# Splitting the Fourier input into halves: reading rows in place and writing with a step, through a small buffer

## The chip, the cores and the metric

The kernel runs on one core of a Trainium2 chip. The metric is the device time of one execution in microseconds (us), taken as the median of several runs.

## The reference

For each of 8 batches of 4224 tokens by 192 channels, a causal convolution with 7 taps per head comes first; it is followed by a two-dimensional Fourier transform of which the real part is kept, a residual sum, a layer norm and a two-layer MLP.

```python
out = np.einsum('hk,bskhg->bshg', w, x_unf)        # w: softmax over the 7 taps of each of 8 heads
x = out.reshape(B, S, D)                           # 8, 4224, 192
X = np.fft.fft(np.fft.fft(x, axis=1), axis=2)
u = x + np.real(X)
un = (u - mu) / np.sqrt(var + 1e-06)               # mu, var over the 192 channels
return u + np.maximum(un @ w_ch1, 0.0) @ w_ch2     # 192 -> 768 -> 192
```

## The kernel before, in words

Almost every matrix product is made of three or five float16 products: a number is split into an upper half (its float16 rounding) and a lower half (what is left, again float16), so that float32 accuracy comes out of float16 matmuls.

**Stages of one batch.** The convolution (`conv_unit`, L440) reads windows of the input, multiplies them by a band matrix and stores the result to a scratch tensor `sc` in DRAM. `load_x` (L530) reads the scratch back as `xs`, 128 partitions by 33 rows of 192 channels, in eight pieces of 4 or 5 rows (`PIECES`, L38): piece 1 has 5 rows, the others have 4. `split_x` (L581) splits a piece into the halves `XH` and `XL`. `stage_a` (L605) multiplies 128-column slices of `XH` and `XL` by the Fourier matrix `F` and evicts `yh` and `yl`. `stage_b` (L630) does the next transform and evicts `V`. `prep` (L715) does the last transform, adds the residual `u`, and computes the layer norm, mostly on POOL. `mlp_hidden` (L839) and `mlp_out` (L863) are the MLP; the first evicts `hh` on ACT (L858) and `hlo` on DVE (L859) out of two PSUM buffers with the tag `h`, the second adds its result to `u` on DVE (L885).

**The split before.** For a piece of n rows of 192 channels, a channel being `t*64 + j` with t in 0..2 and j in 0..63, ACT (L591) multiplies by the batch's scale and writes float16 to `XH`; DVE (L599) then reads `xs` and `XH` and writes the lower half to `XL`. Both walk in the order of `XH`, which is j outside and the 99 numbers (row, t) inside: each instruction writes runs of 12 (or 15) neighbouring float16 numbers and reads float32 numbers that lie 64 elements apart, 256 bytes. An instruction has 768 elements a partition (960 for piece 1).

**Order of the work.** The MLP of the 72 steps (8 batches of 9) sets the pace. The stages of later batches are spread between its units by `front` (L939): the splits of batch 2 and later fall into four steps, two pieces in each, well before the batch's `stage_a`; batch 1 has its own tighter tables (`conv_1` to `a_1`, L931 to L934). `in_turn` (L831) queues an ACT instruction behind the last `hh` eviction emitted before it. Within such limits the framework orders each engine's instructions by a simulated run, in which an engine takes the earliest one in the program that is ready. Each engine then executes its own list strictly in order.

**The head of the program.** For batch 0 there is no MLP to hide behind. `load_first_x` (L549) loads `xs` in four DMAs into the tiles `xs_yh` and `xs_yl`. A tiny POOL copy, `landed` (L578), waits for the last one, and the first residual gathers on POOL (L688) are ordered behind it. For pieces 4 to 7 `split_x` also issues three matmuls into a scratch tile called `idle` (L595), which read that piece's share of `XH`. Then `stage_a` of batch 0 runs; all its matmuls need all eight pieces.

**Buffers.** A tag is a set of slots that tiles share in turn. The tag `hlo` has two slots, used in the head for two input windows and later for the MLP's lower halves. The tag `xl` has one slot, used from batch 2 on by `split_windows` (L403) for the lower half of an input window.

Of the kernel before, what the change touches and what calls it, by code (L numbers as in the profile page):

```python
# [10 lines left out]
F16 = mybir.dt.float16  # L11
# [4 lines left out]
AF = mybir.ActivationFunctionType  # L16
ALU = mybir.AluOpType
# [11 lines left out]
NA, NB, NJ, ND = 128, 33, 64, 3  # L29
NBD = NB * ND  # L30
# [99 lines left out]
def kernel(  # L130
# [13 lines left out]
    nc = tc.nc  # L144
    PSUM = bass.MemoryType.PSUM
    cp = ctx.enter_context(tc.tile_pool(name="cp", bufs=1))
    sb = ctx.enter_context(tc.tile_pool(name="sb", bufs=2))
# [377 lines left out]
    XH = cp.tile([NA, NJ * NBD + 32], F16, name="XH")  # L525
    XL = cp.tile([NA, NJ * NBD + 32], F16, name="XL")
# [53 lines left out]

    def split_x(bt, i):  # L581
        b0, b1 = PIECES[i]
        src = bt.xs.pop(i)[:, : b1 - b0].rearrange("p b (t j) -> p j (b t)", t=ND)

        def part(x):
            return x[:, : NJ * NBD].rearrange("p (j f) -> p j f", f=NBD)[
                :, :, ND * b0 : ND * b1
            ]

        with in_turn():  # L590
            split = nc.scalar.activation(part(XH), src, AF.Copy, scale=bt.c)  # L591
        if bt.b == 0 and i > 3:
            idle = ps.tile([128, HID // 3 * 2], F32, tag="h", name=f"idle_{i}", bufs=2)
            for w in range(3):
                nc.tensor.matmul(  # L595
                    idle[: ND * (b1 - b0)], XH[:, ND * b0 : ND * b1],
                    W1[:, w % 2, : HID // 3 * 2], start=True, stop=True,
                )
        nc.vector.scalar_tensor_tensor(  # L599
            part(XL), src, bt.c, part(XH), op0=ALU.mult, op1=ALU.subtract  # L600
        )
        return split.ins

# [227 lines left out]
    def in_turn():  # L831

        return tc.issue_after(anchor[0]) if anchor[0] else ExitStack()
# [105 lines left out]
    def front(bt, rel):  # L939
        units = []  # L940
        conv, load, split, a = (
            (conv_1, load_1, split_1, a_1) if bt.b == 1
            else (conv_at, load_at, split_at, a_at)
        )
        if bt.b > 1 and rel == min(conv):
            units += [call(split_windows, bt, 0), call(load_windows, bt, 2)]
        for ch in conv.get(rel, ()):
            if bt.b > 1 and ch != conv[rel][0]:
                units += [pause, pause]
            units += [call(conv_unit, bt, ch, p) for p in range(3)]  # L950
            if bt.b > 1 and ch + 1 < NCH:
                units.append(call(split_windows, bt, ch + 1))
            if bt.b > 1 and ch + 3 < NCH:
                units.append(call(load_windows, bt, ch + 3))
        if bt.b > 1 and rel in (min(conv) - 2, min(conv) - 1):
            units.append(call(load_windows, bt, rel - min(conv) + 2))
        if rel == max(conv) - 1 and bt.b >= NB0:
            units.append(call(conv_segments, bt))
        if rel == max(conv) + (bt.b > 1):
            units.append(call(scales, bt))  # L960
        loads = [call(load_x, bt, ch) for ch in load.get(rel, ())]
        splits = [call(split_x, bt, i) for i in split.get(rel, ())]
        for i in range(max(len(loads), len(splits))):
            units += splits[i : i + 1] + loads[i : i + 1]
        units += [call(stage_a, bt, t) for t in a.get(rel, ())]
        return units
# [42 lines left out]
    for i in range(NPC):  # L1009
        split_x(first, i)  # L1010
# [72 lines left out]
    with after(leading["hi"]), after(leading["lo"]):  # L1083
# [3 lines left out]
            op0=ALU.mult, op1=ALU.subtract,  # L1087
        )
    for n in range(len(steps) + 1):
        bt, it = steps[n] if n < len(steps) else (None, 0)  # L1090
# [94 lines left out]
```

## Time and profile before

| what | value |
|---|---|
| three runs | 1221.82, 1225.08, 1227.69 us; median 1225.08 |
| the profiled execution's own time | 1225.67 us |
| its span, first to last instruction | 1223.9 us |
| mean granted TensorE clock | 0.977 |
| busy: PE, DVE, POOL, ACT | 95%, 73%, 66%, 52% |
| instructions of the split: ACT L591, DVE L599 | 64 each |

Engines are named as in the profile: PE is TensorE, DVE VectorE, ACT ScalarE, POOL GpSimd, SP SyncE. "PEclk" is the granted TensorE clock as a share of full speed. A group's row gives the engine, the operation, the tiles out<-in, the shape, the number of instructions, then the busy time in us and the mean ns of one, and last the idle time of the engine just before them and what ended it. In a timeline the first two numbers are the start and the duration in us, and a bracket holds the idle time before and what ended it.

### The profile page before, as it was taken

How to read it: one execution, taken by the hardware profiler on the slowest of the kernel's cores; microseconds unless marked ns; L12 is line 12 of the kernel's file. 1: busy time of each engine (PE TensorE's matmuls, PEld its weight loads, DVE VectorE, ACT ScalarE, POOL GpSimd, SP SyncE). 2: the span in 40 equal slices, each digit the busy share in tenths (PEclk: the TensorE clock that was granted, in tenths of full speed). 3: DMA queues.
4: the chain of work that ended last, by engine and by line, in shares of the span. 5: the costliest groups of instructions: out<-in, count | busy, mean ns of one | idle time of the engine just before them, and what ended most of it. 6: DMA issues, size and time to landing. Idle time of an engine off the chain costs nothing.

```text
span 1223.9 us, 31068 instructions
## 1 busy us (share of the span) xinstructions
PE 1157.8 (95%) x12544; PEld 913.5 (75%) x12544; DVE 894.4 (73%) x2124; ACT 637.6 (52%) x1020; POOL 803.5 (66%) x1104
## 2 busy tenths in 40 slices
PE   4389889999999999999999999999999899999998
PEld 4187668867878778787878778787787777787776
DVE  6767496787767977687867877668778787566543
ACT  5665366555655455654655556554555454333222
POOL 0218965499827896389755897278862899577940
PEclk9589999999999999999999999999999999999999
DMA  8963785474655547384764748466474643323521
GB/s 301 263 187 94 187 184 146 101 182 106 181 142 151 149 126 172 105 191 114 167 170 91 179 105 180 137 153 149 121 175 115 155 106 76 78 69 90 74 56 43
DMA packets 238368, 170.55 MB, mean 139 GB/s; under 512 B 119368, under 2 KB 221968, under 8 KB 238224
## 3 DMA queue, kind: packets, MB, share of 16 engines
q1 hardware_dynamic: 184744, 109.95, 37.4%
q10 hardware_dynamic: 46952, 45.24, 13.2%
q0 software_dynamic: 6528, 13.38, 4.5%
q8 instruction: 98, 1.61, 0.5%
q14 instruction: 46, 0.38, 0.1%
HBM read 83.82 MB, written 58.55 MB: 116 GB/s over the span
## 4 chain that ended last, share of the span: by engine, by line
PE 78%; DVE 8%; DMA 6%; ACT 3%; issue 2%; POOL 1%; SPq 1%; ACTq 0%; DVEq 0%; POOLq 0%
PE ph L854 31%; PE po L879 9%; PE po L873 9%; PE po L876 9%; PE pa L616 6%; PE pq L739 5%; PE pb L642 4%; PE pc L465 4%; DMA xs<-sc 3%; ACT XH L591 2%; DVE XL L599 1%; DMA sc<-xa 1%; DVE yl L625 1%; DMA xs_yl<-sc 1%; PE pc L470 1%
## 5 line engine op out<-in xcount | busy, mean ns | idle before, releaser
L854 PE MATMUL ph<-kt,W 128*128 128x512 f16 (+1 forms) x2160 | 497.9, 363 | 13.8 <-DVE hlo L859 13.3
L858 ACT ACTIVATE hh<-ph 128x512 f16<-128x512 f32 (+1 forms) x400 | 236.5, 593 | 375.7 <-PE ph L854 364.3
L873 PE MATMUL po<-W,hh 128*128 128x192 f16 x1584 | 384.8, 247 | 7.1 <-DVE u L885 7.1
L879 PE MATMUL po<-W,hlo 128*128 128x192 f16 x1584 | 385.3, 247 | 0.0
L876 PE MATMUL po<-W,hh 128*128 128x192 f16 x1584 | 384.7, 247 | 0.0
L859 DVE SCALAR_TENSOR_TENSOR hlo<-ph,hh 128x512 f16<-128x512 f32 (+1 forms) x400 | 269.1, 675 | 122.4 <-ACT hh L858 121.0
L854 PEld LDWEIGHTS <-W 128*128 128x128 f16 x2160 | 192.8, 98 | 153.6 <-issue 15.2
L794 POOL TENSOR_SCALAR un<-u,mv,y 128x192 f32<-128x192 f32 x260 | 280.9, 1088 | 7.8
L876 PEld LDWEIGHTS <-hh 128*128 128x128 f16 x1584 | 155.1, 98 | 28.7 <-issue 8.8
L688 POOL DMA_INDIRECT u<-sc,rows_sb x136 | 155.0, 1140 | 31.4 <-issue 31.2
L873 PEld LDWEIGHTS <-hh 128*128 128x128 f16 x1584 | 155.0, 98 | 23.1 <-issue 0.6
L879 PEld LDWEIGHTS <-hlo 128*128 128x128 f16 x1584 | 155.1, 98 | 18.4 <-issue 0.3
L811 POOL TENSOR_TENSOR hl<-un,hl 128x512 f16<-128x512 f32 (+2 forms) x142 | 131.5, 947 | 5.6
L599 DVE SCALAR_TENSOR_TENSOR XL<-xs,s_x,XH 128x768 f16<-128x768 f32 (+1 forms) x56 | 92.6, 1653 | 43.1 <-ACT XH L591 43.1
L785 POOL TENSOR_SCALAR v<-mv 128x4 f32<-128x4 f32 (+1 forms) x71 | 18.5, 261 | 157.7 <-DVE mv L765 153.4
L757 DVE SCALAR_TENSOR_TENSOR u<-pq,g,u 128x128 f32<-128x128 f32 (+1 forms) x328 | 102.9, 378 | 25.1 <-PE pq L739 20.6
L591 ACT ACTIVATE XH<-xs,s_x 128x768 f16<-128x768 f32 (+1 forms) x56 | 93.9, 1678 | 27.4 <-DMA xs<-sc 27.4
L624 ACT ACTIVATE yh<-pa 99x512 f16<-99x512 f32 x128 | 75.4, 596 | 53.5 <-PE pa L616 43.9
L625 DVE SCALAR_TENSOR_TENSOR yl<-pa,yh 99x512 f16<-99x512 f32 x128 | 85.7, 680 | 23.7 <-ACT yh L624 23.3
L885 DVE SCALAR_TENSOR_TENSOR u<-po,fo,u 128x384 f32<-128x384 f32 (+1 forms) x136 | 80.9, 595 | 27.4 <-PE po L879 26.7
L616 PE MATMUL pa<-c_sb,XH 128*128 128x128 f16 x1024 | 99.6, 221 | 0.0
L739 PE MATMUL pq<-c_sb,V 128*128 128x130 f16 (+1 forms) x1440 | 97.6, 216 | 0.6 <-ACT V L651 0.6
(152 smaller groups left out, 1685.8 us busy)
## 6 DMA issues: line engine op xcount, KB each, us to landing
out_dram<-u SPq DMA_DIRECT2D x64, 384.0 KB
xt<-in_xw_dram ACTq DMA_DIRECT2D x30, 576.0 KB
sc<-xa ACTq DMA_DIRECT2D x30, 540.0 KB
xs<-sc SPq DMA_DIRECT2D x28, 288.0 KB
u<-sc SPq DMA_DIRECT2D x72, 96.0 KB
xt<-in_xw_dram SPq DMA_DIRECT2D x10, 576.0 KB
sc<-xa SPq DMA_DIRECT2D x10, 540.0 KB
xs<-sc SPq DMA_DIRECT2D x28, 192.0 KB
```

Source lines behind the costliest of these rows:

```text
L591: split = nc.scalar.activation(part(XH), src, AF.Copy, scale=bt.c)
L616: nc.tensor.matmul(pa[:, i], x[:, at], F[:, l], start=(n == 0), stop=(n == 2))
L688: nc.gpsimd.indirect_dma_start(to, None, bt.sc[:S], bass.IndirectOffsetOnAxis(ap=rows_sb[:, col : col + 1], axis=0),)
L739: mm = nc.tensor.matmul(po, weights(v, ND * r + k3), rhs[:, 0] if it == Q0 else rhs, start=(r + n == 0), stop=(r == 1 and n == 2),)
L794: (nc.vector if b + it == 0 else nc.gpsimd).tensor_scalar(un[:, g], u[:, g], mv[:, g, 0:1], y[:, g : g + 1], op0=ALU.subtract, op1=ALU.mult,)
L811: lower = (nc.vector if b + it == 0 else nc.gpsimd).tensor_tensor(bl[:, :, o : o + n], un[:, :ng, f], hi[:, :, f], op=ALU.subtract)
L854: nc.tensor.matmul(ph[:, n], W1[:, w, ht * 128 : (ht + 1) * 128], kt[:, k], start=(i == 0), stop=(i == len(order) - 1),)
L858: anchor[0] = nc.scalar.activation(hh, ph, AF.Relu).ins
L859: nc.vector.scalar_tensor_tensor(hlo, ph, 0.0, hh, op0=ALU.max, op1=ALU.subtract)
L873: nc.tensor.matmul(po[:, g % 2], hh[:, ht, tk], W2[:, ht, 0], start=(ht == 0), stop=False)
L876: nc.tensor.matmul(po[:, g % 2], hh[:, ht, tk], W2[:, ht, 1], start=False, stop=False)
L879: nc.tensor.matmul(po[:, g % 2], hlo[:, ht, tk], W2[:, ht, 0], start=False, stop=(ht == 5),)
```

## The change

`split_x` alone is changed. Batch 1 keeps the old form. For the other batches:

- ACT's scaled copy now goes to a new tile `near`, in the order in which the rows lie in `xs`; both its sides are contiguous.
- A second instruction copies `near` to `XH`. It reads in order and writes each float16 number 99 elements (198 bytes) from the one before. For batch 0 it is on POOL, for batches 2 to 7 on ACT.
- DVE reads `xs` and `near`, both in order, and writes `XL` with the same step of 198 bytes.
- `near` takes its slot from the tag `hlo` (two slots) in batch 0 and from the tag `xl` (one slot) from batch 2 on.

The idle matmuls of batch 0 still read `XH`. The layout of `XH` and `XL` and everything that reads them stay as they were.

```diff
     def split_x(bt, i):
         b0, b1 = PIECES[i]
-        src = bt.xs.pop(i)[:, : b1 - b0].rearrange("p b (t j) -> p j (b t)", t=ND)
-
-        def part(x):
-            return x[:, : NJ * NBD].rearrange("p (j f) -> p j f", f=NBD)[
-                :, :, ND * b0 : ND * b1
-            ]
-
+        src = bt.xs.pop(i)[:, : b1 - b0]
+        n = ND * (b1 - b0)
+
+        def part(x, order):
+            return x[:, : NJ * NBD].rearrange("p (j f) -> " + order, f=NBD)
+
+        if bt.b == 1:
...
+        src = src.rearrange("p b (t j) -> p (b t) j", t=ND)
+        hi, lo = (part(x, "p f j")[:, ND * b0 : ND * b1] for x in (XH, XL))
+        tag, bufs = ("xl", 1) if bt.b else ("hlo", 2)
+        near = sb.tile([NA, 5 * ND, NJ], F16, tag=tag, name=f"near_{bt.b}_{i}", bufs=bufs)
+        near = near[:, :n]
         with in_turn():
-            split = nc.scalar.activation(part(XH), src, AF.Copy, scale=bt.c)
+            split = nc.scalar.activation(near, src, AF.Copy, scale=bt.c)
+            if bt.b:
+                nc.scalar.activation(hi, near, AF.Copy)
+            else:
+                nc.gpsimd.tensor_copy(hi, near)
         if bt.b == 0 and i > 3:
...
         nc.vector.scalar_tensor_tensor(
-            part(XL), src, bt.c, part(XH), op0=ALU.mult, op1=ALU.subtract
+            lo, src, bt.c, near, op0=ALU.mult, op1=ALU.subtract
         )
         return split.ins
```

More of the change, by code (lines that the diff above doesn't have):

```diff
@@ L582, in split_x @@
         b0, b1 = PIECES[i]
-        src = bt.xs.pop(i)[:, : b1 - b0].rearrange("p b (t j) -> p j (b t)", t=ND)
-        def part(x):
-            return x[:, : NJ * NBD].rearrange("p (j f) -> p j f", f=NBD)[
-                :, :, ND * b0 : ND * b1
-            ]
-        with in_turn():
-            split = nc.scalar.activation(part(XH), src, AF.Copy, scale=bt.c)
+        src = bt.xs.pop(i)[:, : b1 - b0]
[3 more added lines that the diff above has]
+        if bt.b == 1:
+            src = src.rearrange("p b (t j) -> p j (b t)", t=ND)
+            hi, lo = (part(x, "p j f")[:, :, ND * b0 : ND * b1] for x in (XH, XL))
+            with in_turn():
+                split = nc.scalar.activation(hi, src, AF.Copy, scale=bt.c)
+            nc.vector.scalar_tensor_tensor(
+                lo, src, bt.c, hi, op0=ALU.mult, op1=ALU.subtract
+            )
+            return split.ins
+        src = src.rearrange("p b (t j) -> p (b t) j", t=ND)
[3 more added lines that the diff above has]
+        near = near[:, :n]
+        with in_turn():
+            split = nc.scalar.activation(near, src, AF.Copy, scale=bt.c)
[3 more added lines that the diff above has]
+                nc.gpsimd.tensor_copy(hi, near)
         if bt.b == 0 and i > 3:
```

## The prediction, made before the change was run

> **What bounds the kernel now.** I read the page first, then the stretches of the span, then who waits for whom on PE, then the timeline of the places that the splits touch.
>
> ```profile
> PE 1157.8 (95%) x12544; PEld 913.5 (75%) x12544; DVE 894.4 (73%) x2124; ACT 637.6 (52%) x1020; POOL 803.5 (66%) x1104
> ```
>
> PE is busy for 95% of the span. That alone does not say it is the bound, so I cut the span where PE pauses. The columns are window and length, busy time (and instructions) of PE, PEld, DVE, ACT and POOL, granted clock, DMA share and GB/s:
>
> ```profile
> 240.00:264.00 24.00, 21.31 (x269) 17.83 (x267) 21.52 (x62) 12.46 (x19) 19.82 (x27) 1.00 0.86 203
> 264.00:386.00 122.00, 121.88 (x1342) 95.92 (x1339) 91.35 (x222) 69.63 (x113) 88.43 (x123) 1.00 0.54 138
> 386.00:400.00 14.00, 12.45 (x160) 11.10 (x158) 10.15 (x23) 7.29 (x8) 9.32 (x12) 1.00 0.84 220
> 528.00:542.00 14.00, 13.49 (x176) 12.14 (x173) 10.79 (x24) 8.32 (x10) 10.96 (x14) 1.00 0.99 238
> 670.00:686.00 16.00, 14.31 (x191) 12.96 (x188) 11.46 (x25) 8.69 (x11) 12.97 (x14) 1.00 1.02 228
> 812.00:834.00 22.00, 19.50 (x229) 16.25 (x227) 16.10 (x35) 9.98 (x14) 15.75 (x24) 0.92 0.87 210
> 962.00:980.00 18.00, 14.76 (x154) 11.78 (x153) 14.65 (x36) 8.29 (x11) 16.42 (x22) 0.84 0.73 186
> ```
>
> Between the pauses PE has no gap: 121.88 of 122.00 us at full clock. Nothing that ACT or DVE saves there can be seen in the time. The other six windows are the starts of the splits of batches 2 to 7. There PE idles 2.69, 1.55, 0.51, 1.69, 2.50 and 3.24 us, 12.2 in all, and in the last two the clock falls as well, to 0.92 of 22 us and 0.84 of 18 us, worth another 1.8 and 2.9 us. So the changed splits of the steady part can win 17 us at most, 1.4%. What ends the waits:
>
> ```profile
> PE ph L854 <- DVE hlo L859: 13.3, 6, 3.5
> PE po L873 <- DVE u L885: 7.1, 5, 2.5
> ```
>
> Both are DVE evictions. The start of batch 7's splits shows what holds DVE, ACT's queue first:
>
> ```profile
> 966.35 1.65 ACT L591 ACTIVATE XH<-xs,s_x 128x768 f16<-128x768 f32 x1 [4.34 <-DMA xs<-sc]
> 968.80 1.99 ACT L591 ACTIVATE XH<-xs,s_x 128x960 f16<-128x960 f32 x1 [0.81 <-DMA xs<-sc]
> 970.70 0.89 ACT L651 ACTIVATE V<-pb 128x408 f16<-128x408 f32 x2
> 971.48 0.59 ACT L858 ACTIVATE hh<-ph 128x512 f16<-128x512 f32 x1
> ```
>
> ```profile
> 970.83 2.25 DVE L599 SCALAR_TENSOR_TENSOR XL<-xs,s_x,XH 128x960 f16<-128x960 f32 x1 [0.76 <-ACT XH L591]
> 973.09 0.58 DVE L885 SCALAR_TENSOR_TENSOR u<-po,fo,u 128x384 f32<-128x384 f32 x1
> 973.68 1.04 DVE L653 SCALAR_TENSOR_TENSOR V<-pb,V 128x408 f16<-128x408 f32 x2
> 974.63 0.68 DVE L859 SCALAR_TENSOR_TENSOR hlo<-ph,hh 128x512 f16<-128x512 f32 x1
> ```
>
> The load of piece 1 lands, ACT splits it, DVE takes its lower half, and only then come the `u`, `V` and `hlo` that PE waits for. ACT had `hh` ready at 972.07, 2.56 us before DVE took it up: on this chain DVE is last and ACT has room.
>
> **The head.** Here there is no cover; stage A starts when all eight pieces are split.
>
> ```profile
> 41.57 6.64 ACT L591 ACTIVATE XH<-xs_yh,s_x 128x768 f16<-128x768 f32 x4 [1.85 <-DMA xs_yh<-sc]
> 52.89 3.13 ACT L591 ACTIVATE XH<-xs_yl,s_x 128x768 f16<-128x768 f32 x2 [0.81 <-DMA xs_yl<-sc]
> ```
>
> ```profile
> 50.60 3.05 DVE L599 SCALAR_TENSOR_TENSOR XL<-xs_yl,s_x,XH 128x768 f16<-128x768 f32 x2 [0.69 <-ACT XH L591]
> 54.53 3.04 DVE L599 SCALAR_TENSOR_TENSOR XL<-xs_yl,s_x,XH 128x768 f16<-128x768 f32 x2 [0.89 <-ACT XH L591]
> ```
>
> ```profile
> 54.55 2.96 PE L595 MATMUL idle<-W,XH 128*12 128x512 f16 x6 [0.97 <-ACT XH L591]
> 57.45 1.03 PE L616 MATMUL pa<-c_sb,XH 128*128 128x128 f16 x8
> ```
>
> Both halves are ready at 57.57 (54.53 + 3.04), and the idle matmuls of the last piece end at about the same time. Up to the last landing the loads set the pace: ACT and DVE pause between the pairs.
>
> **Prices.** These rows are groups by shape: count, busy us, mean ns of one.
>
> ```profile
> L591 ACT ACTIVATE XH<-xs,s_x 128x768 f16<-128x768 f32 x49 | 80.0, 1635 | 13.1 <-DMA xs<-sc 13.1
> L309 ACT ACTIVATE W<-w1a,s_w 128x768 f16<-128x768 f32 x1 | 0.9, 936 | 0.1
> L432 ACT ACTIVATE xh<-xt,wc 128x1152 f16<-128x1152 f32 x30 | 37.6, 1252 | 17.7 <-DVE wc L424 17.5
> L599 DVE SCALAR_TENSOR_TENSOR XL<-xs,s_x,XH 128x768 f16<-128x768 f32 x49 | 78.1, 1593 | 33.4 <-ACT XH L591 33.4
> L599 DVE SCALAR_TENSOR_TENSOR XL<-xs,s_x,XH 128x960 f16<-128x960 f32 x7 | 14.5, 2076 | 9.8 <-ACT XH L591 9.8
> L310 DVE SCALAR_TENSOR_TENSOR W<-w1a,s_w,W 128x768 f16<-128x768 f32 x1 | 1.0, 1005 | 0.0
> ```
>
> L309 and L310 do the split's arithmetic on 768 elements with every side contiguous. The stepped read therefore costs ACT 0.70 us (1635 - 936) and DVE 0.59 us (1593 - 1005) an instruction. `near` is L309's case: 0.94 us, and for 960 elements 1.09 (936 and a half of the way to 1252 at 1152). That part is sure. The stepped write is in no row. Its bounds are free (the contiguous row) and as dear as the read (the stepped row); the lower half on DVE is then 1.01 to 1.59 us, for 960 elements 1.26 (1005 times 960/768) to 2.08. I take the upper ends on ACT and DVE: the same engine, count and types, and a step of 198 bytes where 256 was, only on the other side. The lower end speaks for a gain, and I keep it for the range.
>
> The Trainium skill (Vector Engine (DVE) Microarchitecture Reference, section 5.2, Measured stream behaviour on trn2) says that any port which hops on every element slows, read or write: 1.73 ns a column for one hopping source, 1.71 for a hopping destination, and 2.50 for a destination that steps by 24 words. The trace agrees on the read side (1593 ns for 768 columns, 2.07 ns each with the fixed part in it); no run here shows the write. By its 2.50 the lower half would cost an estimated 2.1 us and a pair in the head an estimated 3.6, which is where rival two begins.
>
> **Steady part, batches 2 to 7.** From the landing of piece 1 to the end of its lower half it was 1.98 + 2.08 = 4.05 us; it becomes 1.09 + 2.08 = 3.17, so 0.88 sooner on the chain that PE waits for (1.70 with free writes, 1.09 + 1.26). ACT, on the other hand, is held for `near` and the copy, 1.09 + 1.98 = 3.07 instead of 1.98: `V` and `hh` come 1.1 later, inside their 2.56 us of room. Windows: 0.88 each from four of the six, 0.51 from the one that has no more; in batch 2 piece 0 and piece 1 start 1.8 us apart:
>
> ```profile
> 247.87 1.65 ACT L591 ACTIVATE XH<-xs,s_x 128x768 f16<-128x768 f32 x1 [3.08 <-DMA xs<-sc]
> 249.67 1.97 ACT L591 ACTIVATE XH<-xs,s_x 128x960 f16<-128x960 f32 x1 [0.15 <-DMA xs<-sc]
> ```
>
> The single `near` slot is free only when DVE's lower half of piece 0 is done, at 247.87 + 0.94 + 1.59 = 250.4, which takes away 0.7 of the gain there. Together 4 x 0.88 + 0.51 + 0.1 = 4.1. The pause at 812 falls to 1.6 us, about that at 670 where the clock stayed at 1.00, so I give back its 1.8; the one at 962 falls to 2.36, and of its 2.9 I give back 1.1. Sum: 7.0 us won. With free writes it is 8.8 (1.70 from the windows that have it, all that the others have) and nearly all the clock, 13.4.
>
> Elsewhere ACT has 0.2 to 0.9 us more per split, 48 times: 11 to 45 us of busy time. PE's own work hides it, and without that cover all of it would be paid. The new wait for the `near` slot stops ACT's queue, `hh` included, then `hlo` on DVE and the next `ph` on PE; in the starts shown, batch 2's is the only one where the pieces come closer than a lower half takes. Batch 1 is untouched.
>
> **Head, batch 0.** POOL gets eight copies, and POOL and DVE do not overlap freely:
>
> ```profile
> 52.62 1.03 POOL L578 COPY landed<-xs_yl 128x4 f32<-128x4 f32 x1 [52.19 <-DMA xs_yl<-sc]
> ...
> 817.76 1.96 POOL L808 CAST hl<-un 128x768 f16<-128x768 f32 x1
> ...
> 762.25 0.82 POOL L808 CAST hl<-un 128x768 f16<-128x768 f32 x1
> ```
>
> ```profile
> 817.44 1.64 DVE L599 SCALAR_TENSOR_TENSOR XL<-xs,s_x,XH 128x768 f16<-128x768 f32 x1 [1.09 <-ACT XH L591]
> ```
>
> A copy of 4 elements took 1.03 us and ended at 53.65, exactly when DVE's L599 ended (50.60 + 3.05). The cast that began inside an L599 took 1.96 instead of 0.82. So a POOL copy waits while a lower half runs, and every piece now has one of each, ready at the same moment: they take turns. A copy costs 0.82 us at least; with ACT's ratio of stepped to contiguous (1635/936) it is 1.43, and I take the middle, 1.13, because POOL has no stepped row at all. A pair is 1.59 + 1.13 = 2.72 us, the long piece 3.49. From 42.5 (41.57 + 0.94) eight turns, 7 x 2.72 + 3.49 = 22.5, end at 65.0: no longer the loads but this line of turns sets the end, 7.5 us later than 57.57. With all writes free the pairs are 1.83, the long one 2.29, and the end is 57.6, no loss. With 1.43 it is 67.5, a loss of 10.0, and 1.4 more if the last turn is the copy, for then the idle matmuls of the last piece (half of 2.96) stand behind it on PE and stage A behind them. The gathers queued behind `landed` on POOL may move back as well:
>
> ```profile
> 63.67 0.94 POOL L688 DMA_INDIRECT u<-sc,rows_sb  x1 [0.30 <-issue]
> ```
>
> ```profile
> L757 DVE SCALAR_TENSOR_TENSOR u<-pq,g,u x328: 329/385/420, 76.6 to 1175.1; 128x128 f32<-128x128 f32 x96, 128x192 f32<-128x192 f32 x68
> ```
>
> The last of the first eight ended at 64.6, and DVE first reads their rows at 76.6, a point that moves back with stage A; 12 us cover them. Everything after stage A in the head hangs on it, so the loss is carried to the end.
>
> **Sum.** 1225.67 (the profiled execution; 0.6 above the median) - 7.0 + 7.5 = 1226.2; I forecast 1226 for the median.
>
> **Rivals.**
>
> *One: stepped writes are free.* For it: PSUM evictions with short runs, such as `V` above, show nothing of their layout. Against: the stepped read has its price on both engines. Head 0, steady part -13.4: 1225.67 - 13.4 = 1212.3.
>
> *Two, slower: the stepped write is dearer than the stepped read, and the head's line of turns pays it eight times.* Doubling the extra on each engine gives 1.01 + 2 x 0.59 = 2.18 for the lower half and 0.82 + 2 x 0.61 = 2.04 for POOL's copy; a pair is 4.2, the long one 5.3, and the line ends at 77.3, 19.7 late. The steady gain is gone too (1.09 + 1.26 + 2 x 0.82 = 3.99 against 4.05). 1225.67 + 19.7 = 1245. It decides from about 3.4 us a pair on: then the head loses 13 and the sum is 6 above before.
>
> *Three: the pauses are the loads' and stay.* Each begins with ACT waiting for a landing (4.34 us before 966.35). If a quicker split only lets the next unit wait, the steady part wins nothing and the head still pays: 1225.67 + 7.5 = 1233. Against it: PE's waits end with DVE's work, not with a landing.
>
> **How the numbers follow.** A difference under 0.5%, 6.1 us, cannot be told from none here. Forecast 0.47 (same 0.35, faster 0.06, slower 0.06); rival one 0.25 (faster 0.23, same 0.02); two 0.15 (slower); three 0.13 (slower 0.11, same 0.02). That gives faster 0.29, same 0.39, slower 0.32. The range for 8 in 10 goes from rival one's 1212 to 1238, between two's threshold and its full price; the forecast's own is 1220 to 1232.
>
> **What would show it.** The `near` group on ACT at 0.94 us; the copy to `XH` on ACT between 0.9 and 1.6 and the lower half on DVE between 1.0 and 1.6, which decide between forecast and rivals; in the head, POOL copies and lower halves end to end and the first `pa` near 65 instead of 57.45; PE busy in the six windows up by 4 us and the clock at 812 back at 1.00. A first `pa` at or before 58, or a pause at 962 that has not shrunk, would make the forecast wrong.

## The result, and the profile after

| | before | after |
|---|---|---|
| median | 1226.01 us (4 runs, 1221.82 to 1227.69) | 1340.26 us (4 runs, 1338.31 to 1342.67) |
| the profiled execution: own time, span | 1225.67, 1223.9 us | 1341.14, 1339.4 us |
| mean granted TensorE clock | 0.977 | 0.954 |
| first matmul `pa` of stage A, batch 0 | at 57.45 us | at 102.84 us |

The changed kernel takes 1.0927 times as long, with a 95% interval of 1.0904 to 1.095: 114 us slower. The forecast was no change, and the range ended at 1238. Line numbers of the changed kernel are higher: `near` is L604, the copy to `XH` L606 (ACT) and L608 (POOL), the lower half L616, `pa` L633, `ph` L871, `hh` L875, `hlo` L876.

**The engines.** This is the first part of the page after; before stood at 1157.8, 913.5, 894.4, 637.6 and 803.5 us.

```profile
PE 1176.2 (88%) x12544; PEld 919.4 (69%) x12544; DVE 1030.3 (77%) x2124; ACT 773.5 (58%) x1068; POOL 941.7 (70%) x1112
```

The work is the same 12544 matmuls, yet ACT and DVE are each busy for 136 us more, POOL for 138, and PE's share falls from 95% to 88%. Which instructions got longer is told by the groups by shape (count, then busy us and mean ns of one):

```profile
L604 ACT ACTIVATE near<-xs,s_x 128x768 f16<-128x768 f32 x42 | 39.3, 935 | 7.4 <-DMA xs<-sc 3.6 <-DVE st L781 3.1 <-ACT hh L875 0.5
L606 ACT ACTIVATE XH<-near 128x768 f16<-128x768 f16 x42 | 159.7, 3802 | 1.1
L616 DVE SCALAR_TENSOR_TENSOR XL<-xs,s_x,near 128x768 f16<-128x768 f32 x42 | 165.9, 3949 | 4.6 <-ACT near L604 2.7
L608 POOL COPY XH<-near 128x768 f16<-128x768 f16 x7 | 30.5, 4537 | 46.4 <-ACT near L604 46.4
```

`near`, contiguous on both sides, costs 935 ns, as worked out beforehand. The two instructions that write with a step cost 3.80 us (ACT) and 3.95 us (DVE); those with the old stepped read cost 1.64 and 1.59. This is the first thing to explain.

**Who makes PE wait.** These are the waits of PE's queue (us in total, times, the longest), the costliest of those that changed:

```profile
PE idle L612 <- POOL XH L608: 59.7, 4, 47.6
PE ph L871 <- DVE hlo L876: 33.1, 30, 6.2
PE po L890 <- DVE u L902: 15.4, 5, 3.6
PE po L890 <- ACT hh L875: 7.4, 9, 2.9
```

The waits for `hlo` were 6, together 13.3 us, and are 30, together 33.1; those for `u` went from 7.1 to 15.4 us; a wait for `hh` on ACT is new, and those of the idle matmuls were 14.4 us. So the loss has two places: the head and the splits of batches 2 to 7.

**The head.** POOL, DVE, ACT and PE in turn, from the timeline after (start and duration in us; the bracket is the idle time before and what ended it):

```profile
42.90 17.22 POOL L608 COPY XH<-near 128x768 f16<-128x768 f16 x3 [42.47 <-ACT near L604]
59.70 2.82 POOL L578 COPY landed<-xs_yl 128x4 f32<-128x4 f32 x1
62.70 4.37 POOL L705 DMA_INDIRECT u<-sc,rows_sb  x1 [0.18 <-DMA u<-sc]
...
76.86 0.95 POOL L705 DMA_INDIRECT u<-sc,rows_sb  x1 [0.30 <-issue]
77.82 14.17 POOL L608 COPY XH<-near 128x768 f16<-128x768 f16 x4
95.95 5.46 POOL L608 COPY XH<-near 128x768 f16<-128x768 f16 x1 [3.96 <-ACT near L604]
```

```profile
42.87 23.63 DVE L616 SCALAR_TENSOR_TENSOR XL<-xs_yh,s_x,near 128x768 f16<-128x768 f32 x4 [2.08 <-ACT near L604]
66.08 3.90 DVE L616 SCALAR_TENSOR_TENSOR XL<-xs_yl,s_x,near 128x768 f16<-128x768 f32 x1
82.51 21.77 DVE L616 SCALAR_TENSOR_TENSOR XL<-xs_yl,s_x,near 128x768 f16<-128x768 f32 x3 [12.53 <-ACT near L604]
```

```profile
81.54 0.94 ACT L604 ACTIVATE near<-xs_yl,s_x 128x768 f16<-128x768 f32 x1 [17.53 <-POOL XH L608]
```

```profile
101.47 1.45 PE L612 MATMUL idle<-W,XH 128*12 128x512 f16 x3 [7.97 <-POOL XH L608]
102.84 0.40 PE L633 MATMUL pa<-c_sb,XH 128*128 128x128 f16 x2
```

The first three lower halves run beside POOL's three copies and take 6.57, 8.03 (the long piece) and 6.29 us; the fourth and the fifth, beside `landed` and the gathers, take 3.90 each. POOL does three copies, then `landed`, then the eight gathers to 77.81, and only then the other five copies. Meanwhile DVE has two lower halves to do and then idles 12.5 us, because ACT cannot write the next `near`: both slots are held by pieces that POOL has not copied yet (its 17.53 us of waiting end with a POOL copy). The sixth lower half then lasts 12.36 us, beside three copies that POOL runs one behind the other (DVE and POOL, single instructions of the rows above):

```profile
82.51 12.36 DVE L616 SCALAR_TENSOR_TENSOR XL<-xs_yl,s_x,near 128x768 f16<-128x768 f32 x1 [12.53 <-ACT near L604]
81.08 10.91 POOL L608 COPY XH<-near 128x768 f16<-128x768 f16 x3
```

Stage A starts 45.4 us later than before.

**Batches 2 to 7.** The eight splits of a batch are spread over some 65 us. I cut one such stretch for each batch, six in all, first after and then before (columns as in the prediction; of the six rows the first, the second and the last are shown, then the sum):

```profile
296.00:362.00 66.00, 51.87 (x481) 38.52 (x478) 60.64 (x96) 49.74 (x42) 61.95 (x60) 0.92 0.50 125
451.00:516.00 65.00, 57.58 (x579) 43.83 (x577) 61.51 (x97) 51.80 (x46) 60.61 (x57) 0.97 0.52 133
...
1068.00:1133.00 65.00, 54.89 (x499) 39.82 (x496) 60.10 (x96) 49.84 (x42) 61.03 (x59) 0.92 0.40 102
sum 391.00, PE 337.02 PEld 253.09 DVE 367.02 ACT 306.05 POOL 365.56; mean PE 56.17 PEld 42.18 DVE 61.17 ACT 51.01 POOL 60.93
```

```profile
246.00:312.00 66.00, 63.19 (x666) 48.55 (x664) 54.14 (x124) 37.37 (x52) 60.50 (x77) 1.00 0.57 146
386.00:452.00 66.00, 64.34 (x704) 51.06 (x702) 54.66 (x126) 36.38 (x50) 57.00 (x72) 1.00 0.56 142
...
961.00:1027.00 66.00, 62.76 (x645) 48.28 (x643) 53.59 (x128) 32.98 (x45) 59.95 (x76) 0.95 0.49 116
sum 393.00, PE 380.38 PEld 297.20 DVE 320.86 ACT 212.62 POOL 347.70; mean PE 63.40 PEld 49.53 DVE 53.48 ACT 35.44 POOL 57.95
```

DVE is busy for 367.0 of 391 us, 94%, where it was 320.9 of 393, 82%. PE idles 54.0 us instead of 12.6, 41 more, and the clock was below 1.00 in all six stretches (two at 0.92, four at 0.97: 18 us, against 5 before). Together 54 us. Counted by work, PE did 3285 matmuls in the six stretches instead of 4065; at before's 0.0967 us each the missing 780 are worth 75 us. (The mix of matmuls differs and some records can be missing, so I take 54 and 75 as two rough readings of one loss.) One place in the middle of a stretch shows how it comes about, DVE, ACT and PE in turn:

```profile
487.68 3.80 DVE L616 SCALAR_TENSOR_TENSOR XL<-xs,s_x,near 128x768 f16<-128x768 f32 x1
491.07 0.79 DVE L902 SCALAR_TENSOR_TENSOR u<-po,fo,u 128x384 f32<-128x384 f32 x1
491.76 0.70 DVE L876 SCALAR_TENSOR_TENSOR hlo<-ph,hh 128x512 f16<-128x512 f32 x1
```

```profile
486.73 3.82 ACT L606 ACTIVATE XH<-near 128x768 f16<-128x768 f16 x1
489.98 1.48 ACT L875 ACTIVATE hh<-ph 128x512 f16<-128x512 f32 x2
```

```profile
492.51 1.24 PE L871 MATMUL ph<-kt,W 128*128 128x512 f16 x5 [1.43 <-DVE hlo L876]
```

ACT and DVE write with a step at the same time, each for 3.8 us. `hh` queues behind the one, `u` and `hlo` behind the other, and PE, which has only two PSUM buffers with the tag `h`, waits 1.43 us for `hlo`. No load is involved: this is an ordinary split, neither the first nor the second of its batch.

### The profile page after: what moved, and what is told of

Same layout as the page of the kernel before. It is cut to its first block, busy times and chain, and to the rows that moved or that the text cites. A ratio compares the mean times of both kernels' runs of the same rounds, so it can differ in the third digit from the quotient of the medians.

```text
span 1339.4 us, 31152 instructions
## 1 busy us (share of the span) xinstructions
PE 1176.2 (88%) x12544; PEld 919.4 (69%) x12544; DVE 1030.3 (77%) x2124; ACT 773.5 (58%) x1068; POOL 941.7 (70%) x1112
## 3 DMA queue, kind: packets, MB, share of 16 engines
q10 hardware_dynamic: 46952, 45.24, 12.5%
## 4 chain that ended last, share of the span: by engine, by line
PE 59%; DVE 19%; ACT 7%; issue 5%; DMA 5%; POOL 3%; SPq 1%; ACTq 0%; DVEq 0%; POOLq 0%
PE ph L871 23%; DVE XL L616 7%; PE po L890 6%; PE po L896 6%; PE po L893 6%; PE pa L633 6%; PE pc L465 4%; PE pq L756 4%; PE pb L659 3%; ACT XH L606 3%; DVE hlo L876 3%; DVE u L774 2%; ACT near L604 2%; DVE st L781 1%; DMA sc<-xa 1%
## 5 line engine op out<-in xcount | busy, mean ns | idle before, releaser
L871 PE MATMUL ph<-kt,W 128*128 128x512 f16 (+1 forms) x2160 | 498.8, 364 | 38.5 <-DVE hlo L876 33.1
L875 ACT ACTIVATE hh<-ph 128x512 f16<-128x512 f32 (+1 forms) x400 | 248.9, 630 | 305.4 <-PE ph L871 288.3
L890 PE MATMUL po<-W,hh 128*128 128x192 f16 x1584 | 387.3, 248 | 23.2 <-DVE u L902 15.4
L876 DVE SCALAR_TENSOR_TENSOR hlo<-ph,hh 128x512 f16<-128x512 f32 (+1 forms) x400 | 272.6, 685 | 116.9 <-ACT hh L875 114.0
L871 PEld LDWEIGHTS <-W 128*128 128x128 f16 x2160 | 194.5, 98 | 182.2 <-issue 43.8
L811 POOL TENSOR_SCALAR un<-u,mv,y 128x192 f32<-128x192 f32 x260 | 308.7, 1194 | 7.8
L616 DVE SCALAR_TENSOR_TENSOR XL<-xs,s_x,near 128x768 f16<-128x768 f32 (+1 forms) x48 | 193.8, 4037 | 5.3 <-ACT near L604 3.3
L705 POOL DMA_INDIRECT u<-sc,rows_sb x136 | 166.7, 1226 | 31.5 <-issue 31.0
L606 ACT ACTIVATE XH<-near 128x768 f16<-128x768 f16 (+1 forms) x48 | 187.7, 3910 | 1.3
L828 POOL TENSOR_TENSOR hl<-un,hl 128x512 f16<-128x512 f32 (+2 forms) x142 | 146.7, 1054 | 5.6
L679 POOL COPY V<-V 128x96 f16<-128x96 f16 x64 | 38.9, 609 | 97.7 <-DVE V L670 90.0
L633 PE MATMUL pa<-c_sb,XH 128*128 128x128 f16 x1024 | 101.1, 223 | 3.4 <-ACT XH L606 3.3
L902 DVE SCALAR_TENSOR_TENSOR u<-po,fo,u 128x384 f32<-128x384 f32 (+1 forms) x136 | 84.4, 620 | 18.9 <-PE po L896 17.6
```

The source lines that it names most:

```text
L606: nc.scalar.activation(hi, near, AF.Copy)
L616: nc.vector.scalar_tensor_tensor(lo, src, bt.c, near, op0=ALU.mult, op1=ALU.subtract)
L633: nc.tensor.matmul(pa[:, i], x[:, at], F[:, l], start=(n == 0), stop=(n == 2))
L705: nc.gpsimd.indirect_dma_start(to, None, bt.sc[:S], bass.IndirectOffsetOnAxis(ap=rows_sb[:, col : col + 1], axis=0),)
L811: (nc.vector if b + it == 0 else nc.gpsimd).tensor_scalar(un[:, g], u[:, g], mv[:, g, 0:1], y[:, g : g + 1], op0=ALU.subtract, op1=ALU.mult,)
L828: lower = (nc.vector if b + it == 0 else nc.gpsimd).tensor_tensor(bl[:, :, o : o + n], un[:, :ng, f], hi[:, :, f], op=ALU.subtract)
```

## The experiments

The theory after this reading: a float16 number written on its own, away from the last one, costs some 4.8 ns on any engine, the price is a matter of the bytes written and not of this place, and the two losses follow from it (with POOL's queue and the turns with DVE added in the head). Rivals: the price comes from ACT, DVE and POOL disturbing one another, or from the odd step of 198 bytes; and the loss comes from the new waits for the slots of `near` and not from the price.

**The price by itself.** This kernel computes nothing of the reference: it only runs instructions on 768 elements a partition, alone and in pairs, with many output steps, and writes zeros. An entry gives the type of the output, its step in elements and the neighbours written at each place (0: the order of the changed kernel, 64 places in 12 passes).

```python
    writes = {
        "plain": (F16, 0, 0),
        "hop_iv": (F16, 2, 1),
...
        "hop_case": (F16, 99, 0),
...
        "pair_lxiv": (F16, 32, 2),
...
        "wide_case": (F32, 99, 0),
```

> The kernel leaves out the whole computation and writes zeros as outputs; it only times instructions of 768 elements, first ACT alone, then DVE alone, then POOL alone, each with writes of several steps and two reads with a step, then ACT and DVE at once and DVE and POOL at once. Theory A (a hopping float16 write has a price of its own on every engine): the write with the step of the case, 198 bytes, takes 3.6 to 3.9 us on ACT alone, on DVE alone and on POOL alone, and ACT and DVE at once take no longer than alone. Theory B (the price comes from ACT, DVE and POOL writing at the same time): alone each takes 1.5 to 1.7 us, as the stepped read did, and only the pair at once takes 3.7. Within A, if the price is for a part of a word that must be merged, a float32 write with a hop costs 1.5 to 1.7 us; if it is for every new place, it costs 3.6 to 3.9 as well, and runs of 2 neighbours halve it.

From the groups by shape (mean ns of one after the comma):

```profile
L223 ACT ACTIVATE act_plain<-src 128x768 f16<-128x768 f32 x3 | 2.5, 843 | 0.5 <-DVE src L149 0.5
L223 ACT ACTIVATE act_hop_viii<-src 128x768 f16<-128x768 f32 x3 | 5.7, 1904 | 0.1
L223 ACT ACTIVATE act_hop_case<-src 128x768 f16<-128x768 f32 x3 | 11.1, 3695 | 0.1
L226 DVE SCALAR_TENSOR_TENSOR dve_hop_case<-src_a,near_a 128x768 f16<-128x768 f32 x3 | 10.9, 3646 | 0.1
L231 POOL CAST pool_hop_case<-src_b 128x768 f16<-128x768 f32 x3 | 11.0, 3677 | 0.2
L223 ACT ACTIVATE act_wide_case<-src 128x768 f32<-128x768 f32 x3 | 4.8, 1596 | 0.1
L223 ACT ACTIVATE act_pair_lxiv<-src 128x768 f16<-128x768 f32 x3 | 2.5, 850 | 0.1
L231 POOL COPY both_pool<-near_d 128x768 f16<-128x768 f16 x4 | 23.7, 5926 | 16.3 <-DVE near_d L246 16.1
```

The price does not need another engine at work: alone, the three engines take 3695, 3646 and 3677 ns with the step of the case. It does not depend on the exact step either: on ACT 16, 64, 200 and 256 bytes gave 3596, 3534, 3577 and 3615 ns, and only 8 bytes (1904) and 4 bytes (1054) were cheaper. What matters is what is written at each place. One float16 number costs 4.8 ns (3695/768); a float32 number at the same count and 396 bytes costs 2.1 (1596/768); two neighbouring float16 numbers at every 64 bytes cost nothing (850 against 843). So, from a step of 16 bytes on, it is the lone half of a 4-byte word that is dear, more than twice as dear as a lone word; why it is, no run shows. The stepped read, by its own row in this kernel, was 1489 ns on ACT: as dear as the lone-word write, and not as the write that the change makes. ACT and DVE at once took 3774 and 3718 ns each, 2% more than alone, so they hardly disturb one another. DVE and POOL at once do: a lower half takes 5300 ns and a copy 5926 on average, and four of each take 24.3 us (341.0 to 365.3), 6.1 a pair, where one after the other alone they would take 7.3.

**The two halves of the loss.** The first kernel has the changed split in batches 2 to 7 alone, the second in batch 0 alone; the third is the second with the copy of batch 0 on ACT in place of POOL. The other batches keep the old split.

```diff
-        if bt.b == 1:
+        if bt.b < 2:
```

```diff
-        if bt.b == 1:
+        if bt.b:
```

```diff
-            if bt.b:
-                nc.scalar.activation(hi, near, AF.Copy)
-            else:
-                nc.gpsimd.tensor_copy(hi, near)
+            nc.scalar.activation(hi, near, AF.Copy)
```

> Batch 0 is split in the old form, batches 2 to 7 in the new one. In the changed kernel the first stage A matmul starts at 102.3 instead of 57.45 us, 44.9 later, of 115.5 us in all. If head and steady part add up, this kernel is 65 to 71 us slower than before, about 1294 us. If the steady part only suffers because the head has shifted it against its loads, it is under 20 us slower.

> Batch 0 is split in the new form, all others in the old one. If head and steady part add up: 45 us slower than before, about 1271 us, with the first stage A matmul near 102. If the later batches make up for a late head, less than 30 us slower.

> As head_only, but the stepped copy of batch 0 is on ACT instead of POOL. Theory A with turn-taking and POOL's queue as the second cause: ACT needs 8 times 0.94 + 3.7 and DVE 8 times 3.75, side by side, so that the first stage A matmul comes at 80 to 83 instead of 102 and the kernel takes about 1250 us. If the write price alone were the cause and POOL's queue and the turns nothing, stage A would start at 95 or later and the time would stay near 1270.

Before took 1221.95 us on this chip. Batches 2 to 7 alone: 1286.49, ratio 1.0531 (1.0497 to 1.0565), +64.5 us (65 to 71 expected). Batch 0 alone: 1275.97, ratio 1.0425 (1.0383 to 1.0467), +54.0 us (45 expected). Together 118.5, where the whole change cost 114: within these intervals the two losses add up and nothing else is needed. In the first, the first `pa` is at 58.77, 1.3 us later than in the profile of before, and PE's waits are like those of the changed kernel:

```profile
PE ph L878 <- DVE hlo L883: 38.2, 31, 6.6
```

With the head's copies on ACT (one run, 1253.38 us, +31.4) the first `pa` comes at 80.79 instead of 102.95:

```profile
80.79 0.40 PE L630 MATMUL pa<-c_sb,XH 128*128 128x128 f16 x2
```

There the pace is ACT's alone: eight times `near` and a stepped copy, from 43.60 to 79.36. So of the 45.5 us (102.95 - 57.45) by which the first `pa` is late, 23.3 are left with the copies on ACT (80.79 - 57.45), and 22.2 come with POOL.

**POOL's share of the head.** To part the queue's order from the turns, `landed`, and with it the gathers, was put behind the eighth copy; the rest is the kernel with the changed head alone.

```diff
-        landed = sb.tile([128, 4], F32, tag="v", name="landed", bufs=3)
-        bt.landed = nc.gpsimd.tensor_copy(landed, halves[1][:, 15, :4]).ins
...
-                nc.gpsimd.tensor_copy(hi, near)
+                copied = nc.gpsimd.tensor_copy(hi, near).ins
+                if i == 7:
+                    landed = sb.tile([128, 4], F32, tag="v", name="landed", bufs=3)
+                    with after(copied):
+                        bt.landed = nc.gpsimd.tensor_copy(landed, bt.last_half[:, 15, :4]).ins
```

> The changed split in batch 0 alone, as in the run with the head alone, but the tiny copy landed on POOL is queued behind the eighth copy to XH, so that the eight gathers follow the copies instead of standing in the middle of them. Theory: the head's first pa at 102.95 instead of 57.45 has two parts, POOL's queue (landed and eight gathers, 59.8 to 77.9, while DVE has one lower half to do) and the strict turns of two dear instructions. In the run with the head alone four turns took 23.6 us, 5.9 each; eight of them from 43.0, the long piece a quarter more, end at 43.0 + 7 x 5.9 + 7.4 = 91.7, so the first pa should come at 92 to 95 and the time be 7 to 12 us below that of the head alone, which stood 54 us above before on its chip: about 42 to 47 above before. The price alone (copies on ACT, no turns) gave 80.8. Rival: the queue's order costs nothing, since DVE and POOL would have lost the same time to turns anyway; then the first pa stays at 100 to 104. A second rival: the gathers, now late, hold up the first reads of their rows, and the first pa is early but the time is not.

```profile
42.96 46.72 POOL L607 COPY XH<-near 128x768 f16<-128x768 f16 x8 [42.53 <-ACT near L603]
```

```profile
91.10 0.39 PE L636 MATMUL pa<-c_sb,XH 128*128 128x128 f16 x2
```

Eight copies now run end to end, 5.8 us each, and the first `pa` comes at 91.10, a little before the 92 to 95 expected. (That expectation counted four lower halves of 5.9 us; as said above, three were beside copies and the fourth was not.) The time is 1266.95 us (the profiled execution took 1274.93) against 1225.89, ratio 1.0327 (1.0295 to 1.0359), +41.1 (42 to 47 expected) where the head with the old order had +54.0. Of the 45.5 us, then, 23.3 are there with the copies on ACT, 10.3 come with moving them to POOL, where they and DVE's lower halves hold one another up (91.10 - 80.79), and 11.9 with the order of POOL's queue. These are differences between kernels: on ACT `near` and the copy stand in one queue, on POOL they do not, so 23.3 is not the bare price and 10.3 is what is left of the turns after that relief. The gathers, 29 us later than in the run with the old order, held nothing up that shows. All three head kernels lose 7 to 9 us more than their first `pa` is late (54.0 against 45.5, 31.4 against 23.3, 41.1 against 33.7). In each of them PE has a new wait of 4.8 to 4.9 us for the load of `kt` and one of 2.1 to 2.2 for `hh`, but its waits for `hlo` are 4.7 to 5.3 us shorter (8.0 to 8.6 instead of 13.3), so these do not explain the rest; its cause stays open.

**Which of the two stepped writes costs the steady part.** In batches 2 to 7 alone, the first kernel keeps the stepped copy on ACT and gives DVE its old instruction, which reads `xs` and `XH` across and writes runs of 12; the second keeps DVE's stepped write and gives ACT the old split to `XH`, beside `near`.

```diff
-            lo, src, bt.c, near, op0=ALU.mult, op1=ALU.subtract
+            lo, across, bt.c, hi, op0=ALU.mult, op1=ALU.subtract
```

```diff
-                nc.scalar.activation(hi, near, AF.Copy)
+                nc.scalar.activation(
+                    part(XH, "p j f")[:, :, ND * b0 : ND * b1],
+                    xs.rearrange("p b (t j) -> p j (b t)", t=ND), AF.Copy, scale=bt.c,
+                )
```

> Batches 0 and 1 in the old form. From batch 2 on only ACT writes with the step (contiguous copy, then the stepped copy to XH); DVE takes the lower half in the old order, with the stepped read and the write in runs. ACT is held 0.94 + 3.7 us per split instead of 1.64, and DVE's lower half must wait for the stepped copy. If ACT's stepped copy is what costs the steady part its 64.5 us: 45 to 65 us slower than before. If DVE's stepped write is: under 15 us slower.

> Batches 0 and 1 in the old form. From batch 2 on only DVE writes with the step; ACT makes the contiguous copy for it and writes XH in the old form from the loaded rows, 0.94 + 1.64 us per split. If DVE's stepped write is what costs the steady part its 64.5 us: 35 to 60 us slower than before. If ACT's stepped copy is: under 15 us slower.

Against before's 1228.40 us on this chip: the step on ACT alone 1311.76, ratio 1.0696 (1.0651 to 1.0742), +83 us; the step on DVE alone 1282.96, ratio 1.0454 (1.041 to 1.0498), +55 us. The first is dearer than both together in the earlier run (+64.5). Its row for DVE tells why:

```profile
L626 DVE SCALAR_TENSOR_TENSOR XL<-xs,s_x,XH 128x768 f16<-128x768 f32 x42 | 70.5, 1679 | 116.5 <-ACT XH L614 110.3 <-DMA kt<-hl 3.9 <-issue 2.2
```

DVE is quick again, 1679 ns, but its lower half now reads what ACT's slow copy writes, and DVE, strictly in order, stands still for 110 us behind it with `hlo` and `u` queued. In the changed kernel the lower half reads `near` and does not wait for the copy. So either stepped write is enough to cost over 50 us, they do not add up, and the change's own way of feeding DVE from `near` saves part of the loss. I had expected 45 to 65 us for the first; that wait is the likely difference. POOL shows which step lengthens its own work: it is busy for 892.1 us with the step on DVE and 801.9 with the step on ACT (803.5 before). So of the 138 us by which POOL's work grew in the changed kernel, 37.7 are its eight copies, and most of the rest comes with DVE's step; none of PE's waits shown for batches 2 to 7 ends with POOL.

**The same kernel without the lone halves.** In batches 2 to 7 ACT again goes through `near`, waits for the same slot and issues the same two instructions, but the second copies 384 whole words to places 396 bytes apart instead of 768 half words. `XH` of these batches then holds its numbers in another order; `XL` is made across, from `xs` and `XH`, as before.

```diff
-                nc.scalar.activation(hi, near, AF.Copy)
+                words = XH[:, : NJ * NBD].bitcast(F32).rearrange("p (j f) -> p f j", f=NBD)
+                nc.scalar.activation(
+                    words[:, ND * b0 : ND * b1], near.bitcast(F32), AF.Copy
+                )
```

> As act_steps, but the stepped copy moves two neighbouring float16 numbers as one 4-byte word: 384 words with a hop of 396 bytes in place of 768 halves of a word with a hop of 198. It therefore leaves XH in another order, and the outputs are other numbers; the count of bytes and all other instructions are the same. If a hopping write is dear because it fills only part of a word: the copy takes 0.8 to 0.95 us and the kernel is within 10 us of before. If it is dear for each new place whatever the width: the copy takes 1.8 to 1.9 us (half) and the kernel is 10 to 30 us slower.

```profile
L615 ACT ACTIVATE XH<-near 128x384 f32<-128x384 f32 x42 | 38.4, 914 | 1.4 <-DVE XL L629 0.2
```

The copy takes 914 ns instead of 3754, and the time is 1231.12 against 1228.40 us, ratio 1.0027 (1.0003 to 1.0051), where the kernel with lone halves had 1.0696. There the buffer, its one slot and the extra instruction cost at most half a per cent, so with the step on ACT the loss is the price of the halves. (`near` comes free there with ACT's own copy and not, as in the changed kernel, with DVE's lower half as well; but in the changed kernel ACT idled only 8.6 us in all before the `near` of batches 2 to 7.) For DVE's step there is no such run; its price is read from its rows, 3949 ns in the changed kernel and 3646 alone.

**A layout that has no lone halves.** If whole words are cheap, `XH` and `XL` can be laid out so that channels j and j+1 stand side by side in one word. ACT then writes pairs and reads pairs, in one instruction and without `near`; DVE needs two instructions, one for each half word, with a step of 4 bytes; and stage A loads every second column of 256. This kernel computes all of the reference.

```diff
-        src = bt.xs.pop(i)[:, : b1 - b0].rearrange("p b (t j) -> p j (b t)", t=ND)
+        src = bt.xs.pop(i)[:, : b1 - b0].rearrange("p b (t j r) -> p j (b t) r", t=ND, r=2)
...
+        for r in range(2):
+            nc.vector.scalar_tensor_tensor(
+                part(XL)[..., r], src[..., r], bt.c, part(XH)[..., r],
+                op0=ALU.mult, op1=ALU.subtract,
+            )
```

> Built on the kernel before, for a version that reads and writes in whole words: XH and XL keep channels j and j+1 side by side, so that ACT reads two neighbouring float32 numbers at each hop and writes runs of 24 float16 numbers; DVE does its half in two instructions that read with the old step and write every second float16 number; stage A's weights are then read with a step of 4 bytes. ACT's split falls from 1.64 to 0.95 us, DVE's is 1.6 to 1.8 us as before. If the weight load does not mind the step of 4 bytes: 3 to 6 us faster than before, from the six pauses. If it does, stage A's 1536 loads slow and the kernel is slower, by 150 us if each took 100 ns more on PE's path.

```profile
L591 ACT ACTIVATE XH<-xs,s_x 128x768 f16<-128x768 f32 x49 | 47.6, 971 | 14.7 <-DMA xs<-sc 13.9 <-ACT hh L862 0.7
L600 DVE SCALAR_TENSOR_TENSOR XL<-xs,s_x,XH 128x384 f16<-128x384 f32 x98 | 92.5, 979 | 11.2 <-ACT XH L591 11.2
```

ACT's split falls from 1635 to 971 ns, nearly the whole price of its stepped read (936 with every side contiguous). DVE pays 2 x 979 instead of 1593. The time is 1225.61 us (12 runs, 1221.61 to 1229.98) against 1228.40 (23 runs, 1220.57 to 1233.16), ratio 0.9984 (0.9965 to 1.0004): no difference shown. I had expected 3 to 6 us less; the interval, 4.3 us less to 0.5 more, does not rule out the lower end of that. That fits the reading of before: on the chain of the first pieces ACT gains 0.85 us on piece 1 (1139 ns instead of 1.99 us) and DVE loses 0.2 to 0.4 (2 x 1244 against 2076 to 2250), and everything else lies beside PE's work.

## Why the prediction was wrong

**The price of the stepped write: the step that failed.** The prediction gave it two bounds, "free (the contiguous row) and as dear as the read (the stepped row)", and took the upper ends, "the same engine, count and types, and a step of 198 bytes where 256 was, only on the other side". The other side was not the same: the read takes whole 4-byte words out of their places, the write puts half words into theirs. Measured: 3.80 us for ACT's copy (1.64 taken), 3.95 for the lower half (1.59), 3.68 for POOL's copy alone (1.13). All three lie outside the bounds, and above the 2.18 and 2.04 of rival two, which doubled the extra; on DVE the extra over the contiguous row was five times that of the read (3949 - 1005 = 2944 against 1593 - 1005 = 588 ns). Rival two had the right mechanism for the head and its sign, but not its size.

The Trainium skill (Vector Engine (DVE) Microarchitecture Reference, section 5.2, Measured stream behaviour on trn2), which the prediction cited, gives 1.71 to 2.50 ns a column for a stepping destination and says that it is for 32-bit streams. For 32-bit words at steps of 16 to 396 bytes this chip lies between the two: 1445 to 1555 ns for 768 on DVE, 1.9 to 2.0 each; at 8 bytes the write cost no more than a contiguous one (959 ns each). The write of this kernel is of 16-bit numbers, and the measured 4.7 ns (3646/768) is on no row there. The prediction used that figure without asking whether the number of bytes was the same.

**`near`: right.** 0.94 us forecast, 0.935 measured.

**The steady part: "ACT has room", and the rest is hidden.** The sum looked at the first two pieces of each batch, where PE paused, and put ACT's extra elsewhere at "11 to 45 us of busy time", hidden by PE's work, adding that "without that cover all of it would be paid". With the measured price ACT's extra is 42 x (935 + 3802 - 1635) ns and, for the long pieces, 6 x (1096 + 4659 - 1980), 153 us, and DVE's is 42 x (3949 - 1593) ns and 6 x (4654 - 2076), 114 us. In the six stretches DVE had been idle for 72 of 393 us (393 - 320.9): asked for 114 more, it could not hide them, and PE stopped 30 times for `hlo` instead of six. ACT had been idle for 180 us there (393 - 212.6), more than its 153, and yet the step on ACT alone cost 83 us: what stands behind a long instruction in a strict queue waits, `hh` on ACT itself and, in that kernel, all of DVE's queue. The 2.56 us of room on ACT was right for the place where it was read; a near plus copy of 5.8 us for piece 1 in place of 1.98 is 3.8 longer, past that room. The gain of 7.0 us turned into a loss of 64.5, shown by the kernel with the change in batches 2 to 7 alone.

**The clock.** The forecast of "the clock at 812 back at 1.00" went the other way: with more pauses, all six stretches had a granted clock under 1.00, worth an estimated 18 us (each stretch times what its clock lacks) where 5 had been.

**The head.** That POOL and DVE hold one another up and that this line sets the end was right. In the kernel where `landed` stands behind the copies a pair took 5.8 us, not 2.72, again the price. Strict turns were not kept throughout: the sixth lower half of the changed kernel lasted 12.36 us beside three copies. Two things were left out. First, the order of POOL's list: the prediction moved the gathers back behind the copies, but `landed` and the eight gathers stayed in the middle and the copies 4 to 8 went behind them, which cost 11.9 us. Second, with two slots for `near`, a copy that waits on POOL also stops ACT and then DVE. The first `pa` was forecast near 65 and came at 102.84.

**Rivals one and three** fell with the price: whole words and longer runs can be free to write, lone halves are not, and most of PE's new waits end with DVE's and ACT's work. The one new wait for a landing, 5.2 us for `kt`, is also in the kernel with the changed head alone (4.8), and it is not for the loads of `xs` that rival three meant.

## What to carry to other kernels

Price a stepped access by the bytes at each place and by the side, not by its step: a row for a stepped read of 4-byte numbers says nothing about a stepped write of 2-byte numbers, and an unknown price needs an upper bound that a row really gives, or a range that reaches past it. When a layout must be turned, read with the step and write runs of at least a whole word. And before calling extra time hidden, add it up over the stretch in which it falls and set it against the idle time of that engine there: here 114 us were asked of 72. Fitting into that idle time is not enough, though: ACT's 153 us fitted into 180, and its step alone cost 83.

## What the runs showed of the hardware

- A lone float16 write costs 4.5 to 4.8 ns a number on ACT, DVE and POOL alike (3695, 3646, 3677 ns for 768 at 198 bytes), at every step tried from 16 to 256 bytes; at 8 bytes 2.5 ns (1904), at 4 bytes 1.4 (1054). A lone float32 write costs about 2 ns, the same as a stepped read, and at a step of 8 bytes next to nothing (887 against 843 on ACT).
- Two float16 numbers in one word go at nearly the full rate at steps of 16 and 64 bytes (888 and 850 ns for 768 on ACT, 843 contiguous) and in the kernel with whole words at 396 bytes (914, where the contiguous `near` took 928), and so do runs of 4 and 8 every 64 bytes (842).
- DVE and POOL with these instructions hold one another up: four pairs in 24.3 us, 6.1 a pair, against 3.6 to 3.7 for either alone, but less than the 7.3 that the two take one after the other. Turns are not always even: one lower half lasted 12.36 us beside three copies in a row. The Trainium skill (SBUF — State Buffer, Who interferes with whom) says that a DVE instruction with two SBUF inputs contends with a POOL instruction that reads SBUF; this agrees.
- Stage A's weight load does not mind a step of 4 bytes in its operand. From the groups by shape of the kernel with paired channels; with contiguous columns it was 98 ns:

```profile
L619 PEld LDWEIGHTS <-XH 128*128 128x128 f16 x992 | 79.0, 99 | 11.7 <-issue 2.5
```
